# S4 convolution and gMLP on one core: the program-ordered list of 1214 steps written anew, and five exponential tiles taken from another pool

## The chip, the cores and the metric

The kernel runs on one core of a Trainium2 chip. The metric is device time in microseconds (us), the median of the runs shown. The kernel before took 1722.23 us, the median of three runs (1721.98 to 1733.03).

## The reference

One block on x of shape [2048, 576], with a condition vector c. Two halves follow each other, each with an adaptive LayerNorm: six rows come from silu(c) @ w_mod, three for each half.

```
mod = (silu(c) @ w_mod) in six rows of 576: sa, ca, ga, sb, cb, gb
h = layernorm(x) * (1 + ca) + sa
x = x + ga * S4(h)
h = layernorm(x) * (1 + cb) + sb
x = x + gb * gMLP(h)

S4(u):   dt = exp(log_dt);  l = 0 .. 2047
         K[d, l] = Re sum_n C[d, n] * exp(dt[d] * A[d, n] * l) * dt[d] * B[d, n]     (128 states n, complex A, B, C)
         y = the causal convolution of u with K over l (by FFT of length 4096) + u * Dskip
gMLP(x): z = gelu(x @ w_in)      (576 x 4608);  z1, z2 = its two halves of 2304 columns
         g = w_sp @ layernorm(z2) + b_sp     (w_sp 2048 x 2048, over the tokens)
         (z1 * g) @ w_out
```

## The kernel before, in words

**Three stages.** `body` (line 123) builds an object `Mlp`, then calls `ssm`, `phase_a` and `phase_b`. `ssm` does all of the S4 half and what the gMLP needs for its first token tile. `phase_a` computes z2 for token tiles 1 to 15, and `phase_b` the spatial product, the gate and the output in four blocks. Neither of the two is touched.

**The list.** In `ssm` every piece of work is a small function with the decorator `step`. The constant `ORDER` (line 179) is one list of words such as `e_a.10.1`, and the loop at the end of `ssm` calls the steps in this order. All engines are reached through `Pinned` (line 157): each instruction stays in its engine's queue in the order of the list. So the list sets, for each of PE, DVE, ACT, POOL and SP separately, what stands behind what. An instruction waits at the head of its engine's queue until its inputs are there and its output buffer is free, and all behind it wait too. All these instructions have line 152 in the profile (the call in `Pin`), so they are told apart by the names of their tiles.

**Queues.** A step's transfer is issued by POOL if the step is named in `GPQ` (line 167), else by SP (function `Q`, line 288). POOL issues the stores of the pole terms in any case.

**The opening.** `pole_in` and `pl` prepare the poles of the 576 channels: quarter by quarter of the layout, `pl.0.k` for the first quarter on tiles of 144 columns, `pl.1.k` for the other three together on 432 columns, each in 24 pieces k. Pieces 11, 14 and 22 (`high`) split a value in three bfloat16 parts on ACT and DVE; pieces 12, 15 and 23 (`low`) finish them and store them to `pb_d` and `pa_d`. `pload.c.n` reads them back for a quarter c as tiles `lb` (n 0, exponents), `lc` (n 1) and `la` (n 2, phases; it needs pieces 15 and 23). `m_l`, `m_p`, `m_a`, `m_q`, `m_e` compute the modulation rows 0 to 5: load a slice of w_mod, multiply by silu(c) on PE, fetch the result on ACT (`mpart`), sum it over the partitions with another matmul, and write the rows `gar` (ga), `cga` (ga times 1 + ca), `sga`. `x_l`, `st_a` or `st_v` (statistics on ACT or on DVE), `ln_r`, `ln_p`, `ln_a` are the first LayerNorm with the first stage of the transform of u, stored in `u1_d`.

**The kernel K, 36 groups of 16 channels.** For each group g: `e_p.g.0/1` and `e_a.g.0/1` (matmuls with `lb`, then Exp on ACT into a tile `et` of 1536 columns), `t_p` (matmuls with `lc` and `la`, the phases), `t_i`, `t_b` (to the fraction and its absolute value), `s_f`, `s_c` (Sin on ACT into `ft`), `p_a`, `p_b`, `p_c` (products on DVE into `pg` and back into `et`), `kg_p`, `kg_a`, `kg_d` (16 small matmuls twice, a copy, the skip term), `k1_p`, `k1_e` (first stage of the transform of K). `MODE` (line 165) gives for every group how the phase is reduced: in mode 0, ACT adds a large number and DVE takes the difference, in modes 1 to 4 PE adds and removes the number with more matmuls and the copy is made by DVE (1), by nobody (2), by ACT (3), or Abs is taken on ACT (4). `COPY` (line 166) says whether `k1_e` runs on DVE ("1") or ACT. The pool of `et` has five buffers, that of `ft` three, `pg` two. PSUM tiles come from two buffers of two banks (`ps`) and four of one bank (`pk`).

**The convolution, five chunks c of channels.** `u_l`, `u_p`, `u_a` finish the transform of u, `z_p`, `z_m` multiply it by that of K (chunk c needs `k1_e` of its eight groups), `v_p` and `v_a` make the first inverse stage and store it in `v_d`. When all slices of a chunk are stored, `y_v` reads them back in another layout, `y_x` loads x, `y_p` makes the second inverse stage and `y_s` adds x and stores x1. Chunk 4 is the last and half as wide.

**The turn.** The step `turn` closes the pools of the opening and opens, among others, the pool `wpre`: two buffers of 128 x 2560 float32 called `wst`. Before the change only the steps `wpre.0` and `wpre.1` use them, which load the first two parts of w_in ahead of time. `end` closes the tables of the kernel K.

**The first gMLP steps** are words `ml.*` of the same list. `start_load`, `start_sum`, `start_hi`, `start_lo` (q 0 to 4) load w_in in five parts and build from each a pair of float16 tiles `wz`; `win_scale` computes scales; `ln2_stats`, `roots`, `ln2_rows`, `turn`, `turn_hi`, `turn_lo` are the second LayerNorm of a token tile with its transposition into `nt`; `z2_mm`, `z2_gelu` and `z2_stats` are z2 of token tile 0 (PE, ACT, DVE). The list ends with them, and `phase_a` follows.

Of the kernel before, what the change touches and what calls it, by code (L numbers as in the profile page):

```python
# [166 lines left out]
GPQ = """
c_l.0 c_l.2 c_l.4 c_l.7 cst_l.0 cst_l.1 cst_l.3 ln_a.0.0 ln_a.10.0 ln_a.10.1 ln_a.12.1 ln_a.14.0 ln_a.14.1 ln_a.2.1 ln_a.4.0 ln_a.6.1 ln_a.8.0
ln_a.8.1 m_l.1 m_l.4 ml.ld_l ml.start_load.3 ml.start_x1 ml.turn_lo.0 ml.turn_lo.1 pload.0.2 pload.1.0 pload.1.2 pload.2.0 pload.3.0 pole_in.0.2
pole_in.0.3 pole_in.0.4 pole_in.1.1 pole_in.1.2 pole_in.1.4 pole_in.1.5 pole_in.1.6 r_l.0 r_l.6 st4_l u_a.0.0 u_a.0.4 u_a.0.6 u_a.1.4 u_a.1.6 u_a.1.7  # L170
u_a.2.2 u_a.2.3 u_a.2.4 u_a.2.5 u_a.3.0 u_a.3.2 u_a.3.5 u_a.4.1 u_a.4.3 u_l.0.1 u_l.0.3 u_l.0.4 u_l.0.5 u_l.1.1 u_l.1.2 u_l.1.6 u_l.1.7 u_l.2.0
u_l.2.1 u_l.2.2 u_l.2.3 u_l.2.4 u_l.2.6 u_l.3.0 u_l.3.2 u_l.3.5 u_l.3.7 u_l.4.0 u_l.4.1 u_l.4.3 v_a.0.0 v_a.0.2 v_a.0.6 v_a.0.7 v_a.1.0 v_a.1.4
v_a.1.6 v_a.1.7 v_a.2.0 v_a.2.5 v_a.2.7 v_a.3.2 v_a.3.5 v_a.4.1 v_a.4.2 v_a.4.3 wpre.0 wpre.1 x_l.3 y_s.0.0 y_s.1.0 y_s.1.2 y_s.1.3 y_s.2.1 y_s.2.2
y_s.2.3 y_s.3.0 y_s.3.1 y_s.3.3 y_s.4.0 y_s.4.3 y_v.0.1 y_v.0.2 y_v.0.3 y_v.1.1 y_v.1.2 y_v.1.3 y_v.2.0 y_v.2.1 y_v.2.2 y_v.2.3 y_v.3.0 y_v.3.1
y_v.3.2 y_v.3.3 y_v.4.0 y_v.4.1 y_v.4.2 y_v.4.3 y_x.1.1 y_x.1.3 y_x.2.1 y_x.2.2 y_x.2.3 y_x.3.1 y_x.4.1 y_x.4.2
# [2201 lines left out]
```

## Time and profile before

| what | value |
| --- | --- |
| median of three runs | 1722.23 us |
| profiled execution, its own time | 1726.49 us |
| its span in the trace | 1724.7 us |
| mean granted TensorE clock | 0.974 |
| busy PE, weight loads (PEld), DVE, ACT, POOL | 1647.0, 1244.1, 1239.8, 835.0, 261.6 us |
| data moved | 376.24 MB, mean 218 GB/s |

The profile is of one execution. Times are in us from the start of the span; durations in the rows of groups are the sum of busy time, then the mean of one in ns, then the engine's idle time ahead of the group with what ended it. PE is the matrix engine, PEld its weight loads, DVE the vector engine, ACT the scalar engine, POOL the general engine, SP the engine that only issues transfers. "a<-b" is a result tile and its sources by the program's names. The granted clock is the share of its full clock that PE was given. A row of a stretch of time gives for each engine its busy time and the number of instructions.

### The profile page before, as it was taken

The page shows a single profiled execution, that of the slowest core. Times are in us where ns is not written, and L with a number is a line of the kernel's source. Part 1 is how long each engine was busy: PE and PEld are TensorE (multiplying, and loading weights), DVE is VectorE, ACT ScalarE, POOL GpSimd, SP SyncE. Part 2 cuts the span into 40 slices and gives each one's busy share as a digit, 9 for nine tenths or more (in the row PEclk, how much of TensorE's full clock was granted, in tenths as well). Part 3 has the DMA queues.
Part 4 walks back from the last instruction along what each step waited for, and adds up shares of the span by engine and source line. Part 5 has one row for each costly group of instructions (what it writes and reads, how often), then busy time and mean ns, then how long its engine had stood idle before and what let it go on. Part 6 is the DMA issues. An engine that isn't in the chain of part 4 may idle for free.

```text
span 1724.7 us, 36449 instructions
## 1 busy us (share of the span) xinstructions
PE 1647.0 (95%) x15246; PEld 1244.1 (72%) x15246; DVE 1239.8 (72%) x2187; ACT 835.0 (48%) x1108; POOL 261.6 (15%) x406
## 2 busy tenths in 40 slices
...
GB/s 231 202 209 215 191 191 198 225 282 236 199 284 267 245 240 280 289 263 235 242 158 241 295 269 264 253 208 165 225 224 230 195 222 98 202 200 215 195 99 42
DMA packets 158372, 376.24 MB, mean 218 GB/s; under 512 B 31168, under 2 KB 73536, under 8 KB 157440
## 3 DMA queue, kind: packets, MB, share of 16 engines
...
## 4 chain that ended last, share of the span: by engine, by line
PE 73%; DVE 12%; DMA 8%; ACT 3%; issue 3%; POOL 0%; SPq 0%; ACTq 0%; DVEq 0%; POOLq 0%
PE ps L152 59%; PE pk L152 11%; PE pz L152 3%; DMA zset<-set_d 2%; DVE gt L152 1%; DVE bsz L152 1%; DVE n L152 1%; ACT ft L152 1%; DMA win_d<-wso 1%; DMA wm<-in_w_mod 1%; DMA wst<-in_w_in 1%; DMA u<-u_d 1%; DVE wso L152 1%; DVE rq L152 1%; DVE wsp L152 1%
## 5 line engine op out<-in xcount | busy, mean ns | idle before, releaser
L152 PEld LDWEIGHTS <-zset 128*128 128x128 f16 x7182 | 702.5, 98 | 85.1 <-DMA zset<-set_d 2.2
L152 PE MATMUL ps<-wsp,zset 128*128 128x256 f16 x6048 | 666.4, 273 | 1.2 <-DMA zset<-set_d 1.2
L152 PE MATMUL pz<-wz,nt 128*128 128x512 f16 (+1 forms) x1050 | 208.1, 359 | 0.9 <-DVE nt L152 0.6
L152 ACT ACTIVATE z<-gt 128x1024 f16<-128x1024 f32 x56 | 59.0, 1054 | 282.5 <-DVE gt L152 282.2
L152 PEld LDWEIGHTS <-nt 128*128 128x128 f16 x1120 | 110.6, 100 | 115.6 <-issue 8.3
L2082 POOL DMA_DIRECT2D zset<-set_d x96 | 50.8, 530 | 874.5 <-PE ps L152 626.0
L152 DVE SCALAR_TENSOR_TENSOR gt<-ps,sc,bsp 128x512 f32<-128x512 f32 x36 | 27.0, 750 | 204.1 <-PE ps L152 202.5
L152 PE MATMUL ps<-wout,z 128*128 128x288 f16 x1344 | 170.0, 286 | 0.0
L152 PEld LDWEIGHTS <-z 128*128 128x128 f16 x1344 | 131.5, 98 | 33.0
L152 PE MATMUL ps<-n2o,zset 128*128 128x256 f16 x1134 | 128.2, 273 | 0.0
L152 DVE SCALAR_TENSOR_TENSOR gt<-ps,sc,gt 128x512 f32<-128x512 f32 (+1 forms) x180 | 122.2, 696 | 7.6
L152 DVE TENSOR_TENSOR raw<-raw 128x256 f32<-128x256 f32 (+2 forms) x226 | 117.9, 528 | 12.1 <-DMA raw<-z_d 7.8
L152 ACT ACTIVATE zset<-raw 128x1792 f16<-128x1792 f32 x47 | 79.6, 1696 | 73.9 <-PE ps L152 46.7
L152 DVE TENSOR_TENSOR zset<-raw,zset 128x1792 f16<-128x1792 f32 x47 | 95.0, 2021 | 21.4 <-ACT zset L152 21.3
L152 DVE TENSOR_TENSOR z<-ps,z 128x512 f32<-128x512 f32 (+1 forms) x126 | 71.9, 598 | 36.8 <-ACT z L152 26.7
L152 DVE TENSOR_TENSOR pg<-et,ft 128x1024 f32<-128x1024 f32 x72 | 85.5, 1216 | 5.7 <-ACT ft L152 4.9
L152 PE MATMUL pk<-zz,small 128*128 128x512 f32 x144 | 67.4, 599 | 0.0
L152 ACT ACTIVATE wsp<-raw,sc 128x1792 f16<-128x1792 f32 x25 | 44.6, 1785 | 42.7 <-DVE raw L152 35.0
L152 ACT ACTIVATE z<-z,sc 128x1024 f32<-128x1024 f32 x21 | 24.1, 1148 | 75.6 <-DVE z L152 71.9
L152 ACT ACTIVATE z<-pz,sc 128x512 f32<-128x512 f32 (+1 forms) x90 | 49.3, 579 | 18.8 <-PE pz L152 10.1
L152 PE MATMUL ps<-n2q,wf 128*128 128x512 f16 x252 | 55.9, 379 | 0.0
L152 PE MATMUL ps<-wout,z1b 128*128 128x288 f16 x384 | 52.6, 286 | 1.9 <-ACT z1b L152 1.9
...
## 6 DMA issues: line engine op xcount, KB each, us to landing
...
```

The costliest lines, as they stand in the source:

```text
L152: return self.tc.keep_in_program_order(f(*a, **k))
L2082: self.nc.gpsimd.dma_start(o, self.set_d[f, j - 1] if j else self.wa_d[f])
```

## The change

`ORDER` is written anew as a whole: the same 1214 steps in another order. `GPQ` is another choice of steps (126 instead of 134), `MODE` and `COPY` are other choices, and a new constant `EXTRA` names five groups whose `et` tile comes from the pool `wpre`, 1536 of the 2560 columns of one of its buffers. Lines that begin a stretch of the list, and those in which the steps of the prediction stand:

```diff
@@ -162,86 +162,86 @@
-MODE = [int(k) for k in "314443130422022332040304000000000000"]
-COPY = "000111111111010000110100010000000011"
+EXTRA = [10, 14, 16, 21, 25]
+MODE = [int(k) for k in "334133230244121422400000001002000000"]
+COPY = "000011110010001100010000000011011101"
 GPQ = """
...
 ORDER = """
-pole_in.1.1 pole_in.0.5 pole_in.0.3 pole_in.0.4 pole_in.0.1 pole_in.0.0 pole_in.0.6 load.c pole_in.1.3 pl.0.3 pl.0.0 pole_in.0.2 mod_init load.msk
-pole_in.1.5 pl.0.1 pole_in.1.2 x_l.0 pole_in.1.4 pl.0.4 pl.0.5 pl.0.2 pl.0.11 pl.0.6 pl.0.7 pole_in.1.6 st_a.0.0 pl.0.8 pl.0.9 pl.0.16 pl.0.10 pl.0.13
-st_a.0.1 pl.0.12 pl.0.17 c_l.1 pl.0.18 pl.1.3 m_l.2 pl.0.14 m_p.2 pl.0.19 m_l.0 m_p.0 pl.0.20 st_a.0.2 m_l.1 m_a.2 pl.1.4 pole_in.1.0 pl.1.5 pl.1.6
-pl.1.0 load.small pl.0.21 pl.0.15 st_a.0.3 m_q.2 load.sel pl.1.1 pl.1.7 pl.1.2 m_e.2 m_a.0 pl.0.22 pl.0.23 m_q.0 m_e.0 m_p.1 m_a.1 m_q.1 pload.0.0
-e_p.2.0 st_a.0.4 pl.1.11 e_p.4.1 e_p.0.1 c_l.0 r_l.0 e_a.2.0 m_e.1 ln_r.1 e_p.1.1 e_a.1.1 r_l.1 pload.0.1 pload.0.2 e_p.2.1 t_p.1 ln_r.0 load.dsk
...
-st_v.3.4 p_a.4 p_b.4 m_p.5 m_a.5 kg_d.3 e_a.7.1 p_c.4 kg_p.4 c_l.5 kg_a.4 ln_r.11 ln_p.10.1 k1_p.3 ln_a.10.1 ln_r.12 ln_p.10.0 pl.1.21 pl.1.22
-e_p.10.1 pl.1.23 t_b.5 k1_e.3 ln_a.10.0 e_p.6.0 e_a.10.1 e_a.6.0 r_l.7 ln_r.14 s_f.5 ln_r.15 t_p.6 t_i.6 m_q.5 m_e.5 s_c.5 kg_d.4 ln_r.13 ln_p.12.0
...
-ln_a.12.0 p_a.5 t_b.7 s_f.7 c_l.7 p_b.5 p_c.5 s_c.7 p_a.7 t_b.6 p_b.7 p_c.7 ln_p.12.1 ln_a.12.1 kg_p.5 ln_p.14.0 e_p.11.1 s_c.6 s_f.6 p_a.6 pload.1.2
-ln_a.14.0 e_p.12.1 e_a.12.1 p_b.6 ln_p.14.1 ln_a.14.1 turn cst_l.0 kg_a.5 kg_d.5 p_c.6 kg_p.7 e_a.9.1 u_l.0.4 cst_l.2 t_p.8 t_i.8 t_b.8 e_p.8.0 k1_p.4
-e_a.8.0 s_c.8 k1_p.5 k1_e.4 k1_e.5 pload.1.1 kg_a.7 t_p.9 t_p.10 t_i.10 s_f.8 u_l.0.1 kg_d.7 u_l.0.5 t_i.9 t_b.9 s_c.9 kg_p.6 s_f.9 k1_p.7 u_l.0.0
...
-kg_d.33 u_a.4.2 y_p.1.2 kg_a.34 kg_d.34 k1_e.32 k1_p.33 kg_a.35 k1_p.34 kg_d.35 k1_p.35 k1_e.34 end ml.start ml.start_load.2 k1_e.33 u_l.4.0 y_s.1.2
-ml.ld_l ml.start_sum.1 y_x.4.1 k1_e.35 ml.ld_z z_p.3.7 ml.start_x1 z_p.3.2 u_p.4.3 z_m.3.7 v_p.3.7 ml.start_sum.0 v_a.3.7 z_p.3.1 z_m.3.2 v_p.3.2
...
-y_v.2.1 z_p.4.0 ml.ld_m z_m.4.1 ml.sums v_p.4.1 y_s.2.3 z_m.4.0 y_v.3.0 v_a.4.1 v_p.4.0 v_a.4.0 y_p.2.1 ml.start_hi.1 ml.start_rows y_v.3.1 y_v.3.2
-y_p.2.2 y_s.2.2 y_v.4.0 y_v.4.1 y_p.3.0 y_s.2.1 y_v.3.3 y_p.4.0 y_v.4.2 ml.start_sum.2 y_x.3.0 y_s.3.0 ml.start_lo.1 y_x.4.0 y_s.4.0 y_x.4.2 y_p.4.1
-ml.ap ml.ln2_stats.0 ml.win_scale.7 ml.roots..0 y_p.3.3 y_s.4.1 y_p.3.1 y_x.3.2 ml.start_load.3 y_v.4.3 y_p.4.2 ml.ln2_rows.0 y_s.4.2 y_x.3.1 y_s.3.1
-y_x.3.3 y_p.3.2 y_s.3.2 ml.start_hi.2 y_x.4.3 y_p.4.3 y_s.4.3 y_s.3.3 ml.az ml.turn.0 ml.turn_hi.0 ml.start_lo.2 ml.start_load.4 ml.turn_lo.0
-ml.z2_mm.0.0.0 ml.z2_mm.0.0.1 ml.two ml.start_sum.3 ml.win_scale.8 ml.z2_gelu.0.0 ml.start_hi.3 ml.two_roots ml.ln2_rows.1 ml.z2_mm.0.1 ml.z2_gelu.0.1
-ml.z2_stats.0.0 ml.start_sum.4 ml.z2_mm.0.2 ml.turn.1 ml.start_lo.3 ml.side_load.0 ml.win_scale.9 ml.turn_hi.1 ml.start_hi.4 ml.turn_lo.1
...
+pole_in.0.5 pole_in.0.4 pole_in.0.2 pole_in.0.1 pole_in.0.0 pl.0.0 pole_in.0.3 pole_in.0.6 pole_in.1.5 pole_in.1.0 pole_in.1.1 pl.0.1 pl.0.2 x_l.0
+pl.0.3 pl.0.4 load.msk pl.0.5 pl.0.6 pl.0.11 pl.0.7 pl.0.8 pl.1.0 pl.1.1 pl.0.9 load.c pole_in.1.2 pl.1.2 mod_init st_a.0.0 pl.0.16 pl.0.13 m_l.2
+m_p.2 pl.0.10 pl.0.17 st_a.0.1 st_a.0.2 pl.0.18 pl.0.12 pl.0.14 pl.0.15 m_l.0 m_p.0 st_a.0.3 st_a.0.4 load.small m_a.2 m_q.2 pload.0.0 m_a.0 m_q.0
+pl.0.19 pl.0.20 pl.0.21 m_l.1 pl.0.22 pl.0.23 m_e.2 m_e.0 c_l.1 m_p.1 m_a.1 pole_in.1.3 load.sel e_p.1.0 e_p.3.1 pload.0.1 pl.1.11 m_q.1 m_e.1 e_p.4.1
+r_l.0 ln_r.0 ln_r.1 e_a.1.0 c_l.0 r_l.1 ln_r.3 e_p.1.1 e_a.1.1 pload.0.2 x_l.1 r_l.2 m_l.3 t_p.1 t_i.1 st_v.1.0 st_v.1.1 t_p.0 load.dsk pole_in.1.4
+t_i.0 e_p.2.0 ln_r.2 e_a.2.0 e_p.0.0 e_a.0.0 ln_p.0.0 ln_a.0.0 t_b.0 pole_in.1.6 r_l.3 pl.1.12 ln_p.0.1 t_b.1 s_f.1 ln_a.0.1 pl.1.3 st_v.1.2 pl.1.4
...
+c_l.2 st_v.1.3 st_v.1.4 s_f.0 ln_r.5 ln_p.2.1 ln_a.2.1 ln_r.4 ln_p.2.0 ln_r.6 s_c.0 s_c.1 c_l.3 ln_a.2.0 e_p.0.1 ln_p.4.0 ln_a.4.0 pl.1.5 pl.1.6
+e_a.0.1 x_l.2 ln_p.4.1 ln_a.4.1 pl.1.7 m_p.3 pl.1.8 pl.1.9 p_a.0 m_a.3 t_p.2 t_i.2 t_b.2 p_a.1 pl.1.10 p_b.1 p_c.1 ln_r.7 t_p.3 t_i.3 t_b.3 pl.1.16
...
+p_c.5 ln_p.14.1 ln_a.14.1 pl.1.21 pl.1.22 kg_p.5 p_a.6 pl.1.23 ln_p.14.0 ln_a.14.0 kg_a.5 e_a.9.1 ln_p.12.1 ln_a.12.1 e_p.11.1 e_a.11.1 e_p.8.1 turn
+e_a.14.1 t_p.8 p_a.7 kg_d.4 pload.2.1 e_p.8.0 e_a.8.0 u_l.0.1 u_l.0.5 e_p.12.1 kg_d.5 u_l.0.4 u_l.0.2 t_i.8 p_b.7 p_c.7 e_a.8.1 e_p.9.0 pload.2.2
+e_a.9.0 pload.1.2 p_b.6 p_c.6 t_b.8 s_f.8 k1_p.5 k1_e.5 k1_p.4 k1_e.4 u_l.0.0 s_c.8 t_p.10 t_i.10 t_p.9 t_i.9 cst_l.2 kg_p.6 kg_p.7 t_b.10 t_b.9 p_a.8
+s_f.10 cst_l.0 kg_a.6 kg_d.6 s_c.10 kg_a.7 s_f.9 u_p.0.0 u_a.0.0 p_b.8 p_c.8 u_p.0.1 cst_l.1 k1_p.6 k1_e.6 s_c.9 p_a.9 kg_d.7 u_l.1.2 t_p.12 t_i.12
...
+v_p.3.4 kg_d.34 v_a.3.6 u_p.4.3 s_c.32 v_a.3.4 p_c.35 z_p.3.1 u_a.4.3 z_m.3.1 u_p.3.2 u_l.4.2 s_f.32 p_a.32 p_b.32 u_p.3.5 u_l.4.1 u_a.3.2 z_p.3.2
+u_a.3.5 k1_p.34 p_c.32 k1_p.33 k1_e.33 kg_p.35 k1_e.34 kg_a.35 kg_d.35 kg_p.32 kg_a.32 k1_p.35 u_l.4.0 kg_d.32 k1_p.32 end k1_e.35 ml.start
+ml.start_sum.0 k1_e.32 ml.start_sum.1 ml.start_load.2 z_p.3.5 ml.ld_m v_p.3.1 v_a.3.1 z_m.3.2 z_m.3.5 v_p.3.2 v_a.3.2 ml.start_load.3 ml.win_scale.5.0
+u_p.4.1 u_a.4.1 u_p.4.2 ml.start_hi.0 z_p.3.7 u_a.4.2 ml.sums ml.win_scale.6.0 z_m.3.7 v_p.3.5 ml.start_lo.0 v_a.3.5 z_p.4.3 u_p.4.0 v_p.3.7 z_p.4.1
+ml.start_hi.1 u_a.4.0 v_a.3.7 z_p.4.0 z_m.4.3 v_p.4.3 ml.start_sum.2 z_m.4.1 v_a.4.3 v_p.4.1 y_v.1.2 ml.ld_z ml.start_x1 ml.start_rows z_m.4.0 y_x.4.0
+v_a.4.1 z_p.4.2 z_m.4.2 v_p.4.0 ml.start_sum.3 v_p.4.2 v_a.4.0 ml.start_lo.1 ml.az ml.win_scale.7 v_a.4.2 y_v.4.0 y_v.3.0 ml.win_scale.8 ml.ap
+ml.start_hi.2 y_p.2.2 y_s.2.2 ml.start_lo.2 ml.start_load.4 y_x.1.2 y_v.2.1 y_p.3.0 y_x.3.0 y_s.3.0 y_p.4.0 y_x.3.3 y_s.4.0 ml.ln2_stats.0 ml.roots..0
+y_p.2.1 ml.ld_l y_s.2.1 ml.ln2_rows.0 y_p.1.2 ml.turn.0 y_s.1.2 ml.start_sum.4 ml.two y_x.4.2 ml.turn_hi.0 ml.z2_mm.0.0.0 y_v.3.2 ml.turn_lo.0 y_v.3.1
+ml.two_roots ml.win_scale.9 ml.start_hi.3 ml.start_lo.3 y_v.4.2 ml.ln2_rows.1 y_v.3.3 ml.z2_mm.0.0.1 ml.z2_gelu.0.0 ml.z2_mm.0.1 ml.z2_mm.0.2 y_x.3.2
+ml.z2_gelu.0.1 ml.z2_stats.0.1 y_v.4.1 y_p.3.2 ml.z2_gelu.0.2 ml.z2_stats.0.2 ml.turn.1 ml.start_hi.4 y_s.3.2 y_x.2.3 y_v.4.3 y_p.4.2 y_s.4.2 y_x.3.1
+ml.side_load.0 ml.start_lo.4 ml.z2_mm.0.3 ml.ln2_rows.2 y_v.2.3 ml.turn_hi.1 y_x.4.3 ml.turn_lo.1 ml.ln2_stats.3 ml.z2_gelu.0.3 ml.z2_stats.0.4
+ml.z2_mm.0.4 y_p.3.1 y_x.4.1 y_p.4.1 y_s.4.1 ml.z2_gelu.0.4 ml.z2_stats.0.3 y_s.3.1 y_p.3.3 y_s.3.3 ml.z2_stats.0.0 y_p.4.3 y_s.4.3 y_p.2.3 y_s.2.3
 """.split()
 
 
...
@@ -661,7 +661,8 @@
         def e_a(g, k):
             p = pe.pop((g, k))
             if g not in et:
-                et[g] = tb.tile([128, 1536], F32, name="et", bufs=5), set()
+                et[g] = (pools["wpre"].tile([128, 5, 512], F32, name="wst").rearrange("p k n -> p (k n)")[:, :1536] if g in EXTRA
+                         else tb.tile([128, 1536], F32, name="et", bufs=5)), set()
             e = et[g][0]
             if k == 0:
                 A.activation(e[:, :1024].rearrange("p (h n) -> p h n", h=2), p, AF.Exp)
```

107 lines of the change are left out of this document (50 added, 57 removed).

## The prediction

> **What bounds the kernel now.** I read first the busy time by stages, cut where the work changes: the start, the opening up to the last LayerNorm matmuls, the dense convolution, its end, and the rest.
>
> ```profile
> 0.00:43.00 43.00, 18.91 (x87) 7.19 (x88) 26.12 (x91) 22.19 (x47) 16.27 (x29) 0.97 0.87 230
> 43.00:133.00 90.00, 66.91 (x1015) 35.08 (x1016) 79.49 (x173) 76.88 (x105) 34.44 (x54) 0.71 0.69 210
> 133.00:346.00 213.00, 207.29 (x3279) 136.27 (x3278) 190.94 (x241) 199.58 (x268) 65.58 (x95) 0.98 0.71 202
> 346.00:377.50 31.50, 30.65 (x163) 19.72 (x163) 19.97 (x42) 13.84 (x21) 17.07 (x25) 1.00 0.93 284
> 377.50:389.50 12.00, 5.11 (x77) 4.44 (x76) 6.10 (x11) 5.67 (x5) 10.61 (x15) 0.81 0.93 281
> 389.50:427.60 38.10, 28.97 (x173) 17.21 (x170) 29.87 (x86) 12.93 (x16) 9.01 (x14) 0.72 0.78 226
> 427.60:640.00 212.40, 211.47 (x1116) 109.93 (x1114) 189.26 (x558) 150.49 (x237) 47.99 (x62) 1.00 0.82 251
> ```
>
> The columns are the stretch, its length, busy time of PE, PEld, DVE, ACT and POOL, the granted clock, DMA share and rate. From 427.6 us, where phase_a begins, PE has no idle time (211.47 of 212.40), and the change touches nothing behind it but what is left over at that border. So the question is when phase_a begins. Before it, PE idles 24.1 us at the start, 23.1 to 133, 5.7 in the dense part, and 6.9 + 9.1 = 16.0 between 377.5 and 427.6. In the dense part PE is at 97% and ACT at 94%: there the list can win almost nothing. The chain of waits shows what holds the end:
>
> ```profile
> 377.50 4.63 DMA v_d<-v
> 382.69 4.86 DMA uu<-v_d
> 396.94 6.83 DMA uu<-in_x
> 404.40 2.75 DVE wz L152 x2
> 427.64 6.92 PE pz L152 x28
> ```
>
> The last v tile goes to memory and back (4.63 + 4.86), y_p.4.0 follows, and further on DVE stands behind a load of x that was issued late (6.83) while z2 waits.
>
> **The work itself.** Both lists hold the same 1214 steps; only order, queues (134 against 126 steps on POOL), MODE and COPY differ. MODE 0/1/2/3/4 goes from 17/2/5/6/6 groups to 16/4/6/5/5, COPY from 16 copies on DVE to 14.
>
> ```profile
> L152 ACT ACTIVATE ft<-ps,consts_s 128x1024 f32<-128x1024 f32 x17 | 19.0, 1120 | 0.4 <-PE ps L152 0.4
> L152 ACT ACTIVATE ft<-ps 128x1024 f32<-128x1024 f32 x23 | 23.4, 1026 | 1.6 <-PE ps L152 1.6
> L152 ACT ACTIVATE k<-pk 128x512 f32<-128x512 f32 x20 | 11.8, 603 | 3.0 <-PE pk L152 2.9
> L152 DVE SCALAR_TENSOR_TENSOR ft<-ft,ps 128x1024 f32<-128x1024 f32 x17 | 20.6, 1215 | 3.4 <-ACT ft L152 3.3
> L152 DVE TENSOR_SCALAR ft<-ft 128x1024 int32<-128x1024 int32 x25 | 17.6, 705 | 0.6
> 45.62 1.22 DVE L152 COPY ft<-ps 128x1024 f32<-128x1024 f32 x1
> L152 DVE COPY k<-pk 128x512 f32<-128x512 f32 x16 | 10.9, 685 | 1.1 <-PE pk L152 1.0
> L152 PE MATMUL ps<-sel 48*128 48x512 bf16 x76 | 16.8, 422 | 3.7 <-issue 1.4 <-DVE ft L152 1.1 <-ACT st1o L152 0.6
> L152 ACT ACT_TABLE_LOAD x38 | 48.8, 1283 | 1.9 <-PEq L2366 0.7 <-DVE ft L152 0.5
> L152 ACT ACTIVATE et<-ps 128x1024 f32<-128x1024 f32 x36 | 36.8, 1038 | 1.2 <-PE ps L152 1.1
> L152 ACT ACTIVATE et<-pk 128x512 f32<-128x512 f32 x36 | 21.4, 609 | 2.0 <-PE pk L152 1.8
> ```
>
> ACT: one rounding copy of mode 0 less (1.12), one copy and one Abs less (2 x 1.03), two k copies more (2 x 0.60): -2.0 us. DVE: mode 0 less once (1.215 + 0.705), mode 1 more twice (2 x (1.22 + 0.705)), mode 2 more once (one operation of that copy's size and source, 1.22), mode 3 less once (0.705), two copies less (1.37): +1.1. PE: one more group with the added constant, four matmuls (16.8 / 76 = 0.22 each), and four more of the phases, half as wide, at most 0.22 each: at most +1.8. Table loads: walking the old list and counting each change between Exp, Ln, Arctan, Sin and Gelu on ACT gives 38, the count of the row; the new list gives 38 too. So nothing there. In the dense part PE leads, so the change of work costs +0.5 (between -1, if ACT decides, and +3, twice PE's share).
>
> **Five buffers.** Groups 10, 14, 16, 21 and 25 take their exponential from the pool that otherwise waits for two weight tiles. What they can free is ACT's wait before an exponential, 1.2 + 2.0 us for all 36 groups by the rows above, and most of it is named as PE's result, not a buffer. I take -1, bounds 0 and -3.2. The two weight loads move later in the list, the second one far, but more than a hundred steps still stand between it and its first reader, start_sum.1: nothing.
>
> **The start.** Here the order matters.
>
> ```profile
> 24.48 2.14 PE L152 MATMUL ps<-k,ec 96*32 96x288 f32 x12 [0.72 <-DMA k<-in_w_mod]
> L152 DVE TENSOR_TENSOR t_n_B_re<-t_n_C_re,t_n_C_im 128x432 f32<-128x432 f32 x1 | 0.6, 609 | 0.0
> 30.64 0.78 ACT L152 ACTIVATE st1o<-ln_x,nm 128x576 f32<-128x576 f32 x1 [1.87 <-DVE nm L152]
> 31.94 0.64 ACT L152 ACTIVATE mpart<-ps 128x576 f32<-128x576 f32 x1
> 43.04 0.75 DVE L152 SCALAR_TENSOR_TENSOR cga<-ps,gar 128x576 f32<-128x576 f32 x1
> ```
>
> The modulation matmul m_p.0 ends at 26.6, but ACT fetches it (m_a.0, the mpart copy) only at 31.94, since it stands behind a statistic that waits for DVE, and DVE is busy with the poles of the other three quarters (pl.1, 0.6 us an operation on 432 columns). From there the chain runs to cga (m_e.1) at 43.04 and the first LayerNorm rows. The new list puts pl.1.3 to pl.1.7, eleven operations or about 6 us of DVE, behind m_e.1, and st_a.0.3 ahead of m_a. m_a.0 can then follow its matmul within a microsecond: 31.9 - 27.5 = 4.4 earlier. The loads of w_mod have two 0.2 MB pole loads fewer before them, 0.4 MB at the 230 GB/s of the first row, 1.9 us, and are issued half a microsecond later: at best 1.4 more. I take -4, bounds 0 (w_mod late) and -6.
>
> The poles pushed back come due later. In the new list pl.1.23 stands closer to its first reader, t_p.10, which needs the tile la:
>
> ```profile
> 118.53 3.72 POOL L152 DMA_DIRECT2D pa_d<-pt  x6 [0.85 <-DVE pt L152]
> pa_d<-pt POOLq DMA_DIRECT2D x24, 54.0 KB, 2.8
> 130.60 1.03 POOL L152 DMA_DIRECT2D la<-pa_d  x2
> DMA to landing us min/median/max: 2.5/3.0/4.3
> 140.84 0.27 PE L152 MATMUL ps<-sel,la 48*128 48x256 bf16 x2
> ```
>
> The last two rows are those of la: its landings, and the first matmul of the old list that reads the second quarter (t_p.9). Six stores take 3.7 to issue and 2.8 to land, the load 1.0 to issue and 3.0 to land: 10.5 us, with the longest landing 11.9. The old list had 22.3 between (118.5 to 140.8), with four LayerNorm steps, a modulation step, two kg and two phase steps on PE. The new one has two LayerNorm steps, two k1, five exponential matmuls and one phase step, about half as much, 10 us. PE takes steps in order, so kg_p.6, kg_p.7 and u_p.0.0 stand behind t_p.10, as ACT's t_i.10 with all that follows it. I take +1, bounds 0 and +4 (the longest landing, and two microseconds less of cover).
>
> **The end.** Behind the last k1 the new list has ACT do four things ahead of the last two v copies that stood behind them before: start_hi.1, start_sum.2 and start_sum.3 (each a pass over a weight tile) and the Gelu table (1.3 by the row of table loads), about 8 us:
>
> ```profile
> L152 ACT ACTIVATE wz<-wst 128x2560 f16<-128x2560 f32 x4 | 9.3, 2334 | 0.0
> ```
>
> ACT was busy 13.84 of 31.50 us there, so they fit; in front of the very last copy one of them may show: +1, bounds 0 and +2.5. The round trip of v stays, with no less around it. Then DVE decides, from y_s.4.0 on:
>
> ```profile
> 389.06 0.42 DVE L152 TENSOR_TENSOR xz<-pk,xz 128x256 f32<-128x256 f32 x1 [3.79 <-PE pk L152]
> 390.44 0.16 DVE L152 COPY sc<-pk 128x1 f32<-128x1 f32 x1
> 391.94 0.16 DVE L152 TENSOR_TENSOR sc<-sc 128x1 f32<-128x1 f32 x1
> 404.00 3.60 PE L152 MATMUL pk<-wz,nt 128*128 128x512 f16 x8 [0.69 <-ACT nt L152]
> ```
>
> Old: from 389.06 to the end of z2_mm.0.4 at 427.64, 38.6 us. New: win_scale.7, win_scale.8 (390.44 to 392.1, 1.7 each) and start_lo.2 (from 404.40, 2.75 in the chain and 3.4 in all) now run inside the round trip of v, where DVE was busy 6.1 of 12 us; the y sums of the later rows, among them those that waited for x (6.83), stand behind turn.0. So n2 of token tile 0 is ready about as early as now (1.7 less for win_scale.7, two y sums of about 0.7 more ahead of it), and turn.0 follows at once instead of after the wait: the first z2 matmul about 8 us behind y_s.4.0 instead of 404.0 - 389.1 = 15. DVE had 29.87 us of work in this stretch; 1.7 + 1.7 + 3.4 = 6.8 of it leave. PE was busy 28.97 us in it; two y products (0.9 each) more stand there now, some of them behind the last z2 matmul. The old 38.6 us were 29.9 of DVE and some 8 of its waits, the longest 6.83. If DVE still led and lost the waits alone behind the x load, it would be 38.6 - 6.8 = 31.8; with its work shortened too PE leads, 29 + 1.8 = 31 at the same clock and about 28.6 if most of what the lower clock costs goes too (rows below); if only the work ahead of turn.0 shrinks and another wait comes, 37.5. I take 32.6: -6, bounds -10 and -1. Left over are five y sums and two stores of statistics, 4 us of DVE in phase_a, which is 89% busy there: +1, bounds 0 and +3.
>
> The granted clock of 0.72 in that stretch costs something too.
>
> ```profile
> L152 PE MATMUL pk<-wz,nt 128*128 128x512 f16 x56 | 16.3, 449 | 1.8 <-DVE nt L152 1.0 <-ACT nt L152 0.7
> L152 PE MATMUL pz<-wz,nt 128*128 128x512 f16 x840 | 187.3, 380 | 0.9 <-DVE nt L152 0.6 <-ACT nt L152 0.3
> ```
>
> Tile 0 takes 449 ns a matmul, the other tiles 380: 56 x 69 ns = 3.9 us. [...]
>
> **Sum.** Start -4, poles +1, work +0.5, buffers -1, v copies +1, end -6, leftovers +1: -7.5 us. The profiled execution took 1726.49 (span 1724.7), 4.3 above the median of 1722.23; -7.5 makes 1719.0 of the former and 1714.7 of the latter, which I predict. All favourable bounds together give -20 (1702), all unfavourable +11.5 (1734).
>
> **The rivals.** *More than that:* every wait at both ends goes, start -6, buffers -3.2, end -10: 1703.0. For it: 40 us of idle PE before phase_a that a joint order of both stages could fill. Against: the round trip of v and the loads at the start are latencies that no order removes. *No difference:* w_mod lands as before, and turn.0, which PE takes behind y_p.2.1 and y_p.1.2, waits for their reads of v as DVE waited for x: of the -6 at the end -1 is left, and of the -4 at the start 0, so -7.5 + 5 + 4 = +1.5, or 1723.7. For it: DMA at 93% in 377.5 to 389.5, and 0.87 in the first 43 us. Against: w_mod has fewer bytes ahead of it. *Slower:* the poles. If the 11.9 us of la show in full, since PE, ACT and DVE have run ahead to the point where all of them need t_p.10, the sum is -8.5 + 11.9 = +3.4: 1725.6; it is slower from a wait of 8.5 us on. For it: POOL takes its steps in order too, and a LayerNorm store, which waits for ACT, stands ahead of the six. Against: nothing else stands between the six and la. That the buffers do nothing at all is within the forecast (1 us).
>
> **Chances.** Forecast 0.45 (its own range 1708 to 1720), more 0.18, no difference 0.24, slower 0.13. One per cent, 17.2 us, is about what a measurement here tells from no change: faster than 1705.0 is most of "more" and a tail of the forecast, 0.17; slower than 1739.5 needs the poles to cost over 25 us, 0.07; within, 0.76. The range, 1702 to 1729, leaves out the far ends of both.
>
> **What would show it.** Right: cga near 39 instead of 43.04; dense part with ACT and PE as full as now; 38 table loads; no wait of DVE for uu<-in_x ahead of the first z2 matmul; phase_a's first pz near 420; a PE gap of a microsecond or two before the first matmul with la of the second quarter. Wrong: cga at 43 or later, a PE gap above 8 us at t_p.10, or y_s.4.0 more than 3 us later against the end of the last k1 than now.

## The result and the profile after

The changed kernel takes 1714.98 us (median of 7 runs, 1713.22 to 1715.86). The kernel before, run beside it, takes 1724.31 us. The ratio is 0.9929, with a 95% interval of 0.9908 to 0.9950: faster by 0.7%. Predicted were 1714.7 us in a range of 1702 to 1729. The profiled execution fell from 1726.49 to 1715.01 us, its span from 1724.7 to 1713.2. Two executions of front_new and one of turn_late, in the experiments below, took 3442 us or more, and the medians and ratios there leave them out.

The same stretches as in the prediction, busy time by stage, of the changed kernel:

```profile
0.00:43.00 43.00, 20.49 (x91) 7.55 (x91) 23.66 (x82) 24.05 (x50) 15.57 (x29) 0.95 0.84 219
43.00:133.00 90.00, 66.85 (x1007) 34.36 (x1008) 80.04 (x175) 75.04 (x101) 27.86 (x44) 0.70 0.67 200
133.00:346.00 213.00, 206.79 (x3100) 134.07 (x3099) 194.02 (x240) 197.17 (x265) 66.11 (x99) 0.98 0.71 202
346.00:377.50 31.50, 31.50 (x317) 22.07 (x316) 23.80 (x50) 22.59 (x29) 11.39 (x17) 1.00 0.99 283
377.50:389.50 12.00, 5.22 (x53) 4.06 (x51) 10.52 (x32) 2.60 (x2) 4.85 (x8) 0.75 0.74 221
389.50:427.60 38.10, 35.38 (x277) 21.65 (x278) 34.23 (x97) 15.26 (x21) 17.66 (x24) 0.95 0.92 275
```

Up to 346 us little has changed: PE idles 22.5, 23.2 and 6.2 us where it idled 24.1, 23.1 and 5.7. From 346 on DVE and ACT do more while PE is full (23.80 and 22.59 us of 31.5, before 19.97 and 13.84), DVE fills the wait for v (10.52 of 12), and PE's work comes sooner behind it. Two rows of the tile `pz` give the ends of phase_a, first of the kernel before, then of the changed one (shortest, middle and longest matmul in ns, then first and last start):

```profile
L152 PE MATMUL pz<-wz,nt x1050: 272/379/634, 427.4 to 642.6; 128*128 128x512 f16 x140, 128*128 128x256 f16 x35
```

```profile
L152 PE MATMUL pz<-wz,nt x1050: 272/379/390, 417.5 to 630.9; 128*128 128x512 f16 x140, 128*128 128x256 f16 x35
```

Phase_a begins 9.9 us earlier and ends 11.7 earlier; behind it nothing differs (1082.1 and 1082.3 us to the end). The way to it has three marks: the last v copy on ACT, y_s.4.0 on DVE and the first z2 product on PE. Of the kernel before, the timeline has the first of them, the other two are in the prediction (389.06 and 404.00):

```profile
376.88 0.60 ACT L152 ACTIVATE v<-pk 128x512 f32<-128x512 f32 x1 [1.17 <-PE pk L152]
```

Of the changed kernel (the copy's tile is called `uu` here, since the last slice to be copied is another one):

```profile
377.91 0.60 ACT L152 ACTIVATE uu<-pk 128x512 f32<-128x512 f32 x1 [1.07 <-PE pk L152]
...
387.76 0.42 DVE L152 TENSOR_TENSOR xz<-pk,xz 128x256 f32<-128x256 f32 x1 [0.17 <-PE pk L152]
...
396.12 1.90 PE L152 MATMUL pk<-wz,nt 128*128 128x512 f16 x8 [0.69 <-ACT nt L152]
```

From these marks the 11.5 us between the two spans can be split and laid beside the prediction's terms:

| stretch | before | after | difference | predicted |
| --- | --- | --- | --- | --- |
| start to the last v copy | 376.88 | 377.91 | +1.0 | -2.5 (start -4, poles +1, work +0.5, buffers -1, v copies +1) |
| last v copy to y_s.4.0 | 12.2 | 9.9 | -2.3 | 0 |
| y_s.4.0 to the first pz | 38.3 | 29.7 | -8.6 | -6 |
| phase_a | 215.2 | 213.4 | -1.8 | +1 |
| rest | 1082.1 | 1082.3 | +0.2 | 0 |

The sum was near, -7.5 against -9.3 in the medians, but all that comes ahead of the last v copy gained nothing, and what comes behind it gained more.

The table stands on one execution of each kernel, and its rows are not equally firm. One kernel that was profiled twice (tail_new and tail_again below) took 9.3 and 9.4 us in the second row and 28.1 and 28.0 in the third, but 215.3 and 213.5 in phase_a. The first mark stood at 376.05 and 376.85 in two more profiles whose list is the changed one nearly up to it (turn_late, scales_late). So -2.3 and -8.6 can be trusted; +1.0 and -1.8 are no larger than what one list gives from profile to profile.

### The profile page after: what moved, and what is told of

Same layout as the page of the kernel before. It is cut to its first block, busy times and chain, and to the rows that moved or that the text cites. A ratio compares the mean times of both kernels' runs of the same rounds, so it can differ in the third digit from the quotient of the medians.

```text
span 1713.2 us, 36468 instructions
## 1 busy us (share of the span) xinstructions
PE 1644.2 (96%) x15254; PEld 1242.8 (73%) x15254; DVE 1244.4 (73%) x2187; ACT 833.8 (49%) x1107; POOL 251.0 (15%) x393
## 5 line engine op out<-in xcount | busy, mean ns | idle before, releaser
L152 DVE TENSOR_TENSOR raw<-raw 128x256 f32<-128x256 f32 (+2 forms) x226 | 118.1, 528 | 11.5 <-DMA raw<-z_d 7.3
L152 DVE TENSOR_TENSOR pg<-et,ft 128x1024 f32<-128x1024 f32 x62 | 74.1, 1218 | 5.8 <-ACT ft L152 3.7
L152 ACT ACTIVATE z<-z,sc 128x1024 f32<-128x1024 f32 x21 | 24.1, 1148 | 75.6 <-DVE z L152 71.9
```

The lines of the kernel that those rows point to most:

```text
L152: return self.tc.keep_in_program_order(f(*a, **k))
```

## Experiments

Two theories stood against each other after the result. T: the whole gain is made behind the step `end`. F: the opening and the dense part have their share as predicted. The list can be cut: up to a step that both lists pass, take one list, and what is left in the order of the other. Rows 1.2 and 2.2 of the y steps and slices 4.2 and 4.3 change places in such a list, so that what is in use at the cut fits. In the diffs the list is wrapped anew and cut at both ends, and "..." stands where lines are left out. All ratios are to the kernel before in the same rounds, where it took 1724.31 us (rounds of the changed kernel), 1725.61 (tail_new, front_new, start_new, no_extra), 1724.92 (open_tail, turn_late, scales_late, warm_tail) and 1727.47 (tail_again, poles_off, queues_old, warm_scales). Kernels of different rounds are best compared by their ratios.

| kernel | median us | ratio | 95% interval |
| --- | --- | --- | --- |
| changed kernel | 1714.98 | 0.9929 | 0.9908 to 0.9950 |
| tail_new | 1710.44 | 0.9916 | 0.9894 to 0.9938 |
| tail_again (the same) | 1709.81 | 0.9912 | 0.9894 to 0.9931 |
| front_new | 1734.61 | 1.0057 | 1.0037 to 1.0077 |
| start_new | 1736.37 | 1.0059 | 1.0035 to 1.0083 |
| no_extra | 1740.40 | 1.0086 | 1.0059 to 1.0113 |
| open_tail | 1714.61 | 0.9940 | 0.9922 to 0.9958 |
| turn_late | 1724.97 | 0.9998 | 0.9985 to 1.0011 |
| scales_late | 1724.85 | 0.9988 | 0.9973 to 1.0004 |
| queues_old | 1719.89 | 0.9967 | 0.9953 to 0.9981 |
| poles_off | 1714.39 | 0.9941 | 0.9923 to 0.9959 |
| warm_tail | 1715.13 | 0.9941 | 0.9927 to 0.9956 |
| warm_scales | 1708.74 | 0.9906 | 0.9888 to 0.9925 |

**The new tail alone (tail_new, and tail_again as a measure for later runs).**

```diff
 kg_d.33 u_a.4.2 y_p.1.2 kg_a.34 kg_d.34 k1_e.32 k1_p.33 kg_a.35 k1_p.34 kg_d.35 k1_p.35 k1_e.34 end
-ml.start ml.start_load.2 k1_e.33 u_l.4.0 y_s.1.2 ml.ld_l ml.start_sum.1 y_x.4.1 k1_e.35
+z_p.3.1 y_s.1.2 z_m.3.1 u_p.3.5 z_p.3.2 u_a.3.5 k1_e.33 u_l.4.0 k1_e.35 ml.start ml.start_sum.0
...
```

> The old list, MODE, COPY, queues and et tiles up to the step end; the 150 steps behind it in the new order with the new queues (rows 1.2 and 2.2 of the y steps and slices 4.2 and 4.3 change places, so that the two halves fit). Theory T, the whole gain is made behind end, by DVE and ACT work that moves under the last convolution matmuls and by turn.0 ahead of the late y sums: 8 to 11 us below the kernel before, phase_a's first pz near 418 against 427. Theory F, the opening and the dense part carry their share as predicted (-2.5 in all before the end): 5 to 7 us below, first pz near 420 to 422.

> The kernel of the run tail_new once more, as the measure for the next two on the same chip: 1709 to 1712, and the first exponential within 0.5 us of 43.3 as in three runs with the old opening (43.63, 43.24, 43.38).

Measured: 15 and 18 us below the kernel before in the medians, 14 and 15 by the ratios, as much as the whole change gives or more (the intervals overlap). F, 5 to 7 us, falls. T holds in that the gain is made behind `end`, but its size, 8 to 11 us, was too small: the first pz stands at 410.3. The last stretches of tail_new:

```profile
346.00:377.50 31.50, 27.19 (x134) 18.01 (x134) 24.59 (x65) 24.35 (x28) 13.13 (x19) 1.00 0.83 245
377.50:389.50 12.00, 8.45 (x71) 6.92 (x72) 10.73 (x26) 2.27 (x5) 7.39 (x10) 0.57 0.93 251
389.50:427.60 38.10, 37.38 (x280) 21.32 (x279) 35.87 (x98) 20.06 (x30) 14.15 (x19) 1.00 1.00 297
```

The wait for v begins sooner here, so that PE has 8.45 us of work in the second row and is nearly full in the third. The last v copy begins 5 us before that of the changed kernel:

```profile
372.96 0.60 ACT L152 ACTIVATE uu<-pk 128x512 f32<-128x512 f32 x1 [1.07 <-PE pk L152]
```

**The new front alone (front_new).** The mirror image: the new list, MODE, COPY, EXTRA and queues up to `end`, the old order behind it.

```diff
 u_a.3.5 k1_p.34 p_c.32 k1_p.33 k1_e.33 kg_p.35 k1_e.34 kg_a.35 kg_d.35 kg_p.32 kg_a.32 k1_p.35 u_l.4.0 kg_d.32 k1_p.32 end
-k1_e.35 ml.start ml.start_sum.0 k1_e.32 ml.start_sum.1 ml.start_load.2 z_p.3.5 ml.ld_m
+y_p.2.2 k1_e.32 ml.start ml.start_load.2 y_s.2.2 ml.ld_l ml.start_sum.1 y_x.4.1 k1_e.35
...
```

> The new list, MODE, COPY, EXTRA and queues up to end, the old order and queues behind it (same exchange of rows). Theory T: within 2 us of the kernel before, since cga 2.5 us earlier is used up by the last LayerNorm matmuls (ACT had done 99.1 us of work by 133 us in both traces). Theory F: 2.5 to 5 us below.

Measured: 9 to 10 us above it (the two profiled executions are 4.6 apart), worse than both theories said. The gain that F expected is not there; of T, "the front gives nothing" holds and "it costs nothing" doesn't. The last fetch of a LayerNorm product (tile `st1o`) begins 3.2 us before the old list's 135.9,

```profile
L152 ACT ACTIVATE st1o<-ps x32: 629/649/695, 47.7 to 132.7; 128x576 f32<-128x576 f32 x32
```

but the last v copy begins at 382.00, 5.1 behind. The two halves' ratios don't add up to the change (-15 and +10 against -9.3): part of the 10 us may be the joint, where the old tail orders its v products for another state of the convolution; how much was not measured.

**Opening or dense part (open_tail).** The new opening up to `turn`, the old dense part, the new tail.

```diff
-EXTRA = [10, 14, 16, 21, 25]
+EXTRA = [10, 12]
...
-e_a.14.1 t_p.8 p_a.7 kg_d.4 pload.2.1 e_p.8.0 e_a.8.0 u_l.0.1 u_l.0.5 e_p.12.1
+e_a.8.1 e_p.10.1 e_a.10.1 kg_d.4 p_a.7 p_b.7 p_c.7 pload.1.2 e_p.12.1 e_a.12.1 p_b.6 cst_l.0 kg_d.5
...
```

> The new opening up to the step turn (with its MODE, COPY and queues for the groups begun there), the old dense part up to end, the new tail of the run tail_new; two groups, 10 and 12, take their exponential from the other pool, since the new opening leaves five tiles in use. Theory D, the dense part of the new list is what costs (front_new was 3.2 us ahead of the kernel before at the last ln_a and 5.1 behind at the last v_a): within 2 us of tail_new or up to 3 below, 1708 to 1712. Theory O, the new opening costs (start_new carried its 6 us of delay at the first exponential through to the end): 1714 to 1718.

Measured: 1714.61, on the side of theory O. Beside tail_new and tail_again (0.9916, 0.9912) the new opening costs 4 to 5 us, though the intervals overlap, so the loss is likely and not shown. Its last `st1o` fetch stands at 134.1, 1.1 to 1.7 us before theirs, and its last v copy at 375.58, 1.8 to 2.6 behind theirs. The added line of the diff shows a possible reason: up to `turn` the new opening has not yet done p_b.6, p_a.7, p_b.7 and p_c.7, which the old one has. By an estimate from the profile before (1216 ns for each of the first three, 688 + 684 for the last) those are 5.0 us of DVE work. No run tests this alone.

Beside the changed kernel (0.9929) the old dense part gives the same time as the new one: MODE, COPY and the five buffers together make no difference that these runs can tell. The comparison is not a pure one, since open_tail has the tail of tail_new and keeps the new MODE and COPY for the groups begun in the opening.

**The start alone (start_new).** The new order up to m_e.1, the old one for what is left.

```diff
+pole_in.0.5 pole_in.0.4 pole_in.0.2 pole_in.0.1 pole_in.0.0 pl.0.0 pole_in.0.3
...
+e_p.1.0 e_p.3.1 pload.0.1 pl.1.11 m_q.1 m_e.1
 pole_in.1.4 pole_in.1.6 pl.1.3 pl.1.4 pl.1.5 pl.1.6 pl.1.7 e_p.2.0 e_p.4.1 e_p.0.1
...
```

> The new order and queues only up to m_e.1 (the step that makes cga), then the old order of what is left, with the old MODE and COPY. cga near 40.5 as in the changed kernel in both theories. Theory T: the poles that are put off, pl.1.3 to 1.7, come back as DVE work behind cga, so the time is within 2 us of the kernel before. Theory F: the 2.5 us carry through to the end, 2 to 4 below.

The first part of the expectation fell: cga came at 48.3, not at 40.5. The waits of PE between 30 and 60 us and the transfers between 30 and 50 us say why:

```profile
PE ps L152 <- DMA lb<-pb_d: 7.7, 2, 6.7
```

```profile
lb<-pb_d POOLq DMA_DIRECT2D x2, 108.0 KB, 8.5
```

The tile lb took 8.5 us to land. In the changed kernel it took 2.5:

```profile
DMA to landing us min/median/max: 2.4/2.5/2.5
```

The stretch from 30 to 37 us, in which lb is issued, shows why, first start_new, then the changed kernel (DMA share and GB/s at the end of the row):

```profile
30.00:37.00 7.00, 6.27 (x28) 2.48 (x28) 3.01 (x5) 3.06 (x7) 1.37 (x3) 1.00 1.05 273
```

```profile
30.00:37.00 7.00, 5.68 (x28) 2.44 (x29) 3.02 (x5) 3.06 (x7) 2.50 (x5) 1.00 0.49 143
```

With the old queues SP issues the next slice of w_mod and the next part of x from 21.6 us on, and lb, issued on POOL at 35.42 us, lands while the DMA share is 1.05 (30 to 37 us) and 0.97 (37 to 45); the new list has both on POOL, behind lb. e_p.1.0 waits for lb and stands ahead of m_q.1 on PE. So the run doesn't tell T from F. It does show that a delay in the opening is not absorbed: 6.1 us at the first exponential, 8.1 at the last v copy, 7.8 at the end of the span.

**One edit of the start (poles_off).** tail_new with the poles that the new list puts off, put off.

```diff
-st_a.0.1 pl.0.12 pl.0.17 c_l.1 pl.0.18 pl.1.3 m_l.2 pl.0.14 m_p.2 pl.0.19 m_l.0 m_p.0 pl.0.20 st_a.0.2 m_l.1 m_a.2 pl.1.4 pole_in.1.0 pl.1.5 pl.1.6
+st_a.0.1 pl.0.12 pl.0.17 c_l.1 pl.0.18 m_l.2 pl.0.14 m_p.2 pl.0.19 m_l.0 m_p.0 pl.0.20 st_a.0.2 m_l.1 m_a.2 pole_in.1.0
...
-ln_a.2.0 ln_p.0.0 ln_a.0.0 s_c.1 pl.1.8 pl.1.10 ln_p.2.1
+ln_a.2.0 ln_p.0.0 ln_a.0.0 s_c.1 pl.1.3 pl.1.4 pl.1.5 pl.1.6 pl.1.7 pl.1.8 pl.1.10 ln_p.2.1
```

> tail_new with one edit in the opening: pl.1.3 to pl.1.7 moved from ahead of m_a.0 to behind ln_a.0.0, as the new list has it; nothing else of the new opening. In both theories the first exponential comes 2 to 4 us earlier than 43.3. Theory W, the 6 us of DVE work come back before the last LayerNorm matmul, where DVE is 88% busy: the last ln_a within 1 us of the old 135.8 and the time within 1.5 us of tail_new. Theory S, as the prediction had it, the chain to cga sets the opening's end: the last ln_a 2 to 4 us earlier and the time 2 to 4 us below tail_new.

Measured: 4.6 us above tail_again, with intervals that just overlap. The first exponential came only 0.9 us earlier (42.4 against 43.3), and the last `st1o` fetch 3.7 us later, 139.5 against 135.8:

```profile
L152 ACT ACTIVATE st1o<-ps x32: 629/644/658, 51.8 to 139.5; 128x576 f32<-128x576 f32 x32
```

The earlier exponential, small as it is, did not carry on, as theory S needs. W was right that the DVE work comes back, wrong that it comes back for nothing. In its timeline DVE works through the poles without a gap, and the tables of LayerNorm wait behind them (the waits of PE and ACT between 43 and 137 us):

```profile
49.30 0.60 DVE L152 TENSOR_TENSOR t_wr<-t_n_C_re,t_n_B_re 128x432 f32<-128x432 f32 x1
...
55.02 2.85 DVE L152 RECIPROCAL t_rnd<-t_n_B_re 128x432 f32<-128x432 f32 x1
```

```profile
PE ps L152 <- DVE rt L152: 4.6, 1, 4.6
```

```profile
ACT ft L152 <- DVE ft L152: 6.1, 3, 4.4
```

**The new list without the second pool (no_extra).**

```diff
-EXTRA = [10, 14, 16, 21, 25]
+EXTRA = []
...
 e_a.14.1 t_p.8 p_a.7 kg_d.4 pload.2.1 e_p.8.0
-e_a.8.0
 u_l.0.1 u_l.0.5
...
+e_a.8.0 e_a.8.1 t_p.9 t_i.9 kg_p.7
...
```

> The new list with all exponentials in the five et buffers: as it would need seven at once, each exponential that finds none free is put off in the list, with what depends on it, until one is. If the two more buffers matter: 3 us or more above the changed kernel, with ACT waiting in the dense part. If they do nothing (as the old list, which has the same dense part without them, suggests): within 2 us of it, 7 to 11 below the kernel before.

Measured: 25 us above the changed kernel (27 by the ratios). PE waits for exponentials (first row: those of the tiles `ps` up to 430 us, 2.4 us in the changed kernel; second: the stretch where it is worst):

```profile
PE ps L152 <- ACT et L152: 9.1, 10, 4.4
```

```profile
200.00:250.00 50.00, 43.47 (x535) 26.64 (x535) 32.90 (x39) 40.13 (x51) 5.99 (x11) 0.85 0.30 88
```

The new order of the dense part needs the buffers. That the buffers make anything faster doesn't follow, since the old order, which needs only five, does as well in open_tail. What the buffers alone would give the old order was not tried: its exponentials are listed so that five suffice.

**What makes the end short (turn_late, scales_late).** Two edits of the changed kernel's tail, each of which undoes one thing.

```diff
 ml.ln2_rows.0 y_p.1.2
+y_x.4.2 y_v.3.2 y_v.3.1 y_v.4.2 y_x.3.2 y_p.3.2 y_s.3.2 y_p.4.2 y_s.4.2 y_x.3.1 y_p.3.1 y_s.3.1
 ml.turn.0 y_s.1.2 ml.start_sum.4 ml.two
```

> The changed kernel with the y steps of rows 3.1, 3.2 and 4.2 (loads, products and sums) put ahead of turn.0, as all late rows were before. If turn.0 ahead of them is what shortens the end: the first z2 matmul 14 us or more behind y_s.4.0 instead of 8.4, and 4 to 7 us above the changed kernel. If PE leads there, which has to do these products in any case: within 2 us of it.

```diff
-y_v.4.0 y_v.3.0 ml.win_scale.8 ml.ap ml.start_hi.2 y_p.2.2 y_s.2.2 ml.start_lo.2 ml.start_load.4 y_x.1.2
+y_v.4.0 y_v.3.0 ml.ap y_p.2.2 y_s.2.2 y_x.1.2
...
+ml.start_hi.2 ml.turn.0 y_s.1.2 ml.two y_x.4.2 ml.turn_hi.0 ml.start_lo.2 ml.start_load.4 ml.z2_mm.0.0.0
```

> The changed kernel with win_scale.7, start_hi.2, start_lo.2 and win_scale.8 put back to the places that they had in the old list, behind ln2_stats.0, ahead of turn.0, behind turn_hi.0 and behind the first z2 products, and with them parts 3 and 4 of w_in, which need their buffers. If the 6.8 us of DVE work that leave the stretch are what shortens the end: 4 to 7 us above the changed kernel. If DVE has slack there: within 2 us.

Measured: 10 to 12 us and 10 us above the changed kernel; each takes back the whole gain, and that is more than was expected. In the kernel before DVE waits for x like this behind 370 us:

```profile
DVE uu L152 <- DMA uu<-in_x: 5.6, 2, 5.4
```

In turn_late the waits of DVE and of PE behind 370 and 340 us are this one, twice as long, and one for v:

```profile
DVE uu L152 <- DMA uu<-in_x: 11.6, 1, 11.6
```

```profile
PE pk L152 <- DMA u<-v_d: 10.2, 2, 10.0
```

In turn_late the first z2 product comes 21.5 us behind y_s.4.0. In scales_late DVE works only 4.32 of 12 us in the wait for v, and PE waits later, for n on DVE and for a weight tile on ACT:

```profile
377.50:389.50 12.00, 5.59 (x65) 4.50 (x62) 4.32 (x16) 0.36 (x1) 6.09 (x8) 0.86 0.86 243
```

```profile
PE ps L152 <- DVE n L152: 3.4, 1, 3.4
PE pk L152 <- ACT wz L152: 3.0, 1, 3.0
```

The first z2 product of scales_late is hardly late, 18.8 us behind the start of the last v copy (18.2 in the changed kernel); the loss lies behind it, 29.6 us to the first pz instead of 21.4. So the two are needed together: the early scales gain only if z2 may start, and an early start of z2 gains only if its weight tiles are ready. A part of either loss goes with the clock, 0.73 from 389.5 to 427.6 us in turn_late and 0.82 in scales_late where the changed kernel had 0.95: the 56 z2 products of tile 0 took 14.7 us in turn_late and 17.4 in scales_late, 12.6 in the changed kernel.

**The way of v (queues_old).** The changed kernel with the old queues for 20 steps behind `end`.

```diff
-GPQ: v_a.3.1 v_a.3.7 v_a.4.0 y_x.1.2 y_x.3.0 y_x.3.2 y_x.4.3 y_s.4.1
+GPQ: v_a.3.2 v_a.3.5 v_a.4.3 y_v.4.0 y_v.2.1 y_v.3.3 y_x.4.2 y_x.2.3 y_s.1.2 y_s.3.1 y_s.3.3 y_s.2.3
```

> The changed kernel with the old queues for the v stores, the v reads, the x loads and the x1 stores behind end (20 steps change between SP and POOL, y_v.4.0 among them from SP to POOL). If spreading the reads of v over both queues is what shortened the way from the last v copy to y_s.4.0 (11.6 us before, 9.3 in the changed kernel): that way 1.5 us longer or more, and 1.5 to 4 us above the changed kernel. If the transfers themselves set it: within 1.5 us.

Measured: 5 to 7 us above the changed kernel, and from the end of the last v copy (374.60) to y_s.4.0 (387.3) 12.7 us instead of 9.3 (11.6 in the kernel before). PE waits 8.4 us for the first read of v where the changed kernel waits 5.0 (queues_old first):

```profile
PE pk L152 <- DMA zz<-v_d: 8.4, 1, 8.4
```

```profile
PE pk L152 <- DMA zz<-v_d: 5.0, 2, 4.6
```

**The clock behind the wait (warm_tail, warm_scales).** tail_new with extra matmuls into a tile that nothing reads.

```diff
+        @step
+        def warm(n):
+            pm = ps2()
+            for i in range(n):
+                T.matmul(pm[:, i % 2], ones, small.rearrange("p a b -> p (a b)")[:, :512], start=True, stop=True)
...
-ml.start_sum.3 v_p.4.3 v_a.4.0 ml.start_lo.1 ml.az ml.win_scale.7 v_a.4.3 y_v.4.0 y_v.3.0 ml.win_scale.8
+ml.start_sum.3 v_p.4.3 warm.8 v_a.4.0 ml.start_lo.1 ml.az ml.win_scale.7 v_a.4.3 y_v.4.0 y_v.3.0 ml.win_scale.8
```

> tail_new with eight extra matmuls of 128x512 in float32 (0.6 us each by the row of the v products) behind the last v product, into a tile that nothing reads: PE then works through most of its 5.3 us of waiting for v. If the lower clock behind the gap costs time (0.57 in 377.5 to 389.5, where PE works 8.45 us): the clock there at 0.9 or more and 2 to 3 us below tail_new. If DVE or the transfers lead there: within 1 us of tail_new or above.

> As warm_tail, but with five extra matmuls, put behind the matmul of win_scale.8, so that no scale stands behind them on PE (in warm_tail DVE waited 5.8 us for one). If the lower clock behind the gap costs time: 1 to 3 us below tail_new. If it doesn't lead: within 1 us of it, with a higher clock in 377.5 to 389.5.

In warm_scales `warm.5` stands behind ml.win_scale.8 instead. warm_tail came out 4 to 5 us above tail_new. Its clock did rise, from 0.57 in tail_new to 0.93 in 377.5 to 389.5, but the matmuls of the two scales stood behind the extra ones, and DVE waited for them (behind 370 us):

```profile
377.50:389.50 12.00, 6.80 (x74) 4.88 (x72) 8.68 (x31) 2.00 (x1) 2.16 (x4) 0.93 0.47 126
```

```profile
DVE sc L152 <- PE pk L152: 5.8, 1, 5.8
```

warm_scales, without that fault, is 1.1 us below tail_again with a clock of 0.72 there (tail_again 0.57); the intervals overlap, so no gain is shown. It and tail_new have the lowest medians of the study, by the ratios 4 us and 2 to 3 us below the changed kernel, with intervals that overlap.

## Why the prediction was right, and where it was not

**The end** was right in its mechanism and too small. The prediction said that turn.0 follows n2 at once, the first z2 product some 8 us behind y_s.4.0 (8.4 by the rows above), since 6.8 us of DVE work move into the wait for v (DVE 10.52 us busy there) and the late y sums behind turn.0. turn_late and scales_late show that both are needed, and DVE's wait for uu<-in_x ahead of the first z2 product is gone, as forecast. One reading was off: the 6.83 us that the prediction takes for DVE's longest wait are the transfer in the chain, and DVE stood idle for 5.4 of them. The term -6 measured -8.6. The clock, 1.00 from 396 to 417.5 us where the kernel before had 0.79 from 404 to 427.4, is enough for the missing 2.6: the prediction took 31 to 37.5 us by the old tile 0, whose products took 449 ns each, and now they take what those of phase_a take:

```profile
L152 PE MATMUL pk<-wz,nt 128*128 128x512 f16 x56 | 12.6, 380 | 1.1 <-ACT nt L152 0.7 <-DVE nt L152 0.4
```

That is 16.3 - 12.6 = 3.7 us of PE in a stretch where PE and DVE are both nearly full (20.3 and 20.2 of 21.5 us busy from 396 to 417.5). Kernels with the same tail list show how much of it comes through: from y_s.4.0 to the first pz took 28.0 to 28.5 us in tail_new, tail_again and poles_off, where these products took 12.6 us, and 29.9 in open_tail, where they took 14.8 (clock from 389.5 to 427.6 us: 1.00, 1.00, 0.97, and 0.91 in open_tail). The prediction put what the lower clock costs at 3.9 us and has no term for it in its sum. The wait for v did stay, and the clock was 0.75 from 377.5 to 389.5 us and 0.68 from there to 396; but, 0.50 from 391 to 393 us, it stood at 1.00 from 393.9 on, and the first z2 product starts at 396.12. In the kernel before it was 0.50 from 400 to 412 us, and z2 began there at 404.00. Ahead of the full clock lie 4.26 us of products without a pause:

```profile
389.63 4.26 PE L152 MATMUL pk<-u,st 128*64 128x128 f32 x32 [1.91 <-DVE rq L152]
```

That these products brought it back is an inference from this one trace. The runs show only that the extra matmuls of warm_tail and warm_scales went with a higher clock from 377.5 to 389.5 us, 0.93 and 0.72 against 0.57 in tail_new and tail_again; how much work it takes was not measured.

**"The round trip of v stays"** failed as a step: 12.2 us became 9.9. The old list issued all its late reads of v behind one another on POOL (375.4 to 392.8 us in its trace); the new one spreads them over POOL and SP, y_v.4.0 on SP. queues_old shows that the queues set it. The other profiles agree: from the start of the last v copy to y_s.4.0 took 12.0 to 13.3 us in the four with the old queues there and 8.8 to 9.9 in eight with the new ones (in warm_tail DVE was held up by the extra matmuls). Which of the 20 steps matters was not tried.

**The start, -4, is the step that failed, though not at its first links.** "m_a.0 can then follow its matmul, 4.4 earlier": in the changed kernel's profile m_a.0 came 2.4 us earlier and cga 2.5. Six more profiles have the same list and queues up to `turn` (front_new, open_tail, no_extra, turn_late, scales_late, queues_old): cga came 2.8 to 4.2 us earlier in five of them and 0.6 in no_extra. In front_new it stands where the prediction had it:

```profile
38.86 0.75 DVE L152 SCALAR_TENSOR_TENSOR cga<-ps,gar 128x576 f32<-128x576 f32 x1
```

So what failed is that the time is kept from there to the end of the convolution. The next link was not looked at. In the changed kernel's timeline DVE has cga at 40.54 and then stands still:

```profile
40.54 0.75 DVE L152 SCALAR_TENSOR_TENSOR cga<-ps,gar 128x576 f32<-128x576 f32 x1
41.33 0.82 DVE L152 SCALAR_TENSOR_TENSOR ln_x<-ln_x,nm,cga 128x576 f32<-128x576 f32 x1
44.80 0.26 DVE L152 TENSOR_SCALAR rt<-r1t,r 128x64 f32<-128x64 f32 x1 [2.65 <-DMA r1t<-in_c_r1t]
```

The kernel before makes its first such table (`rt`) at 44.56, so here the gain is gone in one step; in the six others the table begins between 41.30 and 44.96, so that at most 3.3 us are left. Three loads, of the table r1t, the next part of x and a pole input, now come too late for DVE; between 38 and 133 us they cost

```profile
DVE rt L152 <- DMA r1t<-in_c_r1t: 2.7, 1, 2.7
DVE bs L152 <- DMA ln_x<-in_x: 1.9, 1, 1.9
DVE t_wr L152 <- DMA t_n_B_re<-in_A_B_re: 1.1, 1, 1.1
```

5.7 us together, and 3.6 to 5.4 in the six others; in the old list DVE waited 0.3 for the first and not for the others. Two of them stand on POOL behind the load of lb, which waits 6.7 us there for the pole stores to land:

```profile
34.50 1.04 POOL L152 DMA_DIRECT2D lb<-pb_d  x2 [6.70 <-DMA pb_d<-pt]
...
39.16 0.57 POOL L152 DMA_DIRECT2D r1t<-in_c_r1t  x1
39.72 0.54 POOL L152 DMA_DIRECT2D ln_x<-in_x  x1
```

Besides, the six us of pole work return on an engine that is 88% busy: poles_off shows what that costs, 3.5 us at the last v copy (377.27 against 373.82 in tail_again). The prediction priced one reader of the poles, la, and not the DVE work itself.

Nor does an earlier end of the opening mean as much work done: the last `st1o` fetch stands between 132.7 and 136.6 in the seven profiles and between 134.1 and 135.9 in five with the old opening, but the new list reaches `turn` with the 5.0 us of DVE products of open_tail undone. At the last v copy the balance is a loss: 376.05 to 377.91 in the changed kernel, turn_late and scales_late, 374.00 in queues_old, whose v stores take other queues, and 372.96 to 373.82 in four profiles of the old front with the new tail (tail_new, tail_again, warm_tail, warm_scales). Where -3.5 was forecast for the front (start, poles, work and buffers), it gives about 0 to +5.

**The poles** (+1) were nearly free: PE waited 0.3 us for la (waits of PE up to 430 us), and that rival is out.

```profile
PE ps L152 <- DMA la<-pa_d: 0.3, 1, 0.3
```

**The rivals.** "More" asked for the waits at both ends to go; only some of those at the end did. "No difference" had turn.0 wait on PE behind the reads of v; the changed list avoids that, and turn_late, which brings it back, shows its price.

**Work and buffers** (+0.5 and -1): not told from zero in open_tail. **The v copies** (+1): the table's +1.0 doesn't show this cost. tail_new has the same three passes of ACT ahead of its last v copies, and its last copy begins 3.9 us before that of the kernel before (376.88); some 2.4 of that lie ahead of `end`, where both lists are the same (last skip term, kg_d.35, at 342.4 against 344.8), so no cost is seen. **Leftovers** (+1): no cost is seen here either, but -1.8 isn't a gain of the change: phase_a took 213.8 us in front_new and start_new, which have the old tail, 213.4 in the changed kernel, and 215.3 and 213.5 in tail_new and tail_again, which are one kernel.

The total came out because an opening that was credited with too much and an end that was credited with too little cancelled, and that is luck. Left open: how much of the opening's loss is the three loads, how much the order of the pole work and how much the products left for later; listing r_l.0 and pole_in.1.4 earlier in the new opening was not tried.
